# The tail of a fused attention and SwiGLU backward pass: row sums on ScalarE, another order for the last weight gradient, loads cut in quarters

## The chip, the cores and the metric

The kernel runs on one core of a Trainium2 chip. The metric is the device time of one execution in microseconds (us). Three executions of the kernel before took 1677.09, 1677.39 and 1687.07 us; their median is 1677.39. A fourth execution was taken by the hardware profiler.

## The reference

The forward pass is `x + A(xn) + B(xn)`, with `xn = layernorm(x)` over rows of D = 448, S = 2048 rows. A is attention with 16 heads of 28; B is a SwiGLU block with F = 1792. The kernel computes the output and, from `grad_out`, the gradients of x and of the five weight matrices:

```python
xn = _layernorm(x, axis=-1)
return x + _A_ref(xn, A_wqkv, A_wo) + _B_ref(xn, B_w_gate, B_w_up, B_w_down)
...
_out, _vjp = jax.vjp(_f, A_x, A_wqkv, A_wo, B_w_gate, B_w_up, B_w_down)
_grads = _vjp(grad_out)
```

Two of these results are finished in the tail that the change touches:

- the gradient of `wqkv`, which is `xn^T` times the gradient of queries, keys and values;
- the gradient of x. With g the gradient that reaches xn, one row of it is `rstd * (g - mean(g) - xn * mean(g * xn)) + dy`, so each row needs the sum of g and the sum of g * xn.

## The kernel before, in words

The work is cut into 16 row tiles of 128 rows (t) and 4 groups of four heads (g). A forward part (lines 497 to 548) computes attention, with the SwiGLU block's matmuls filled in between. A backward part (lines 764 to 859) runs over pairs of heads, blocks of keys and queries; into it go jobs such as the output rows, the two SwiGLU parts of the input gradient (stored in DRAM as pA_d and pB_d, rows of 448 in bf16) and the wqkv gradient of groups 0, 1 and 2. Every engine executes its instructions in the order in which the program issues them; nothing reorders them. SP issues most DMAs, POOL many stores, ScalarE one large load. Waits are semaphores that the framework derives from tiles: a buffer of a pool (`bufs=3` means three) is reused only when its readers are done. DMAs take eight semaphores in turn, so a DMA also waits for the one that had its semaphore eight DMAs earlier.

The tail is lines 865 to 921:

- **Loads.** `dy_t` (all 16 tiles of grad_out, 1792 KB) is loaded in one DMA from ScalarE's queue (L870). `pab` holds pA and pB for all tiles, each loaded in two halves of 896 KB by SP (L874). `dq_c`, three buffers, holds the gradient of queries, keys and values of two row tiles (768 KB); chunk ck is loaded at L880, chunks 0 and 1 ahead of everything, chunk t/2 + 2 at each even t.
- **The last wqkv gradient (group 3).** For each of four row blocks c of the weight (128 rows of D), `dwq_mms` (L615) issues 32 matmuls for keys and values (kvm, L622) and then 32 for queries (qm, L627) into one PSUM tile; they read `dkv_sp` and `dq_sp`, transposed by DMA at L707 and L765. `dwq_out` (L634) copies the result on ScalarE (L637), sorts it on POOL (L644) and stores it from POOL (L645). So block 0's queries stand ahead of block 1's keys and values.
- **The tile loop, t = 0 to 15.** TensorE adds pA and pB by two matmuls with an identity (L896) and 12 matmuls of dq_c with the transposed wqkv (L898) in a PSUM tile (pool ps_sd, three buffers of two banks). VectorE copies it to `g_sb` and sums it (s1, L902), multiplies it with xn and sums that (junk, s2, L906), makes the two columns bb and cc (L910, L912); ScalarE computes `t1 = g_sb * rstd + bb` (L915); VectorE adds `xn * cc` (t2, L917); POOL adds dy (dx, L920); SP stores dx (L921).

Nothing overlaps two tiles on VectorE except by order: the next tile's L902 is issued after this tile's L917, which waits for ScalarE.

Of the kernel before, what the change touches and what calls it, by code (L numbers as in the profile page):

```python
# [9 lines left out]
ACT = mybir.ActivationFunctionType  # L10
ALU = mybir.AluOpType
AX = mybir.AxisListType
FP32 = mybir.dt.float32
BF16 = mybir.dt.bfloat16
# [4 lines left out]
D = 448  # L19
# [3 lines left out]
G = 4  # L23
HP = 32
P = 128
NT = S // P
# [11 lines left out]
def kernel(  # L38
# [19 lines left out]
    pe, act, dve, pool, sp = nc.tensor, nc.scalar, nc.vector, nc.gpsimd, nc.sync  # L58
    ctx.enter_context(tc.manual_schedule())
    x_d = A_x.rearrange("b (t p) d -> p (b t) d", p=P)  # L60
    dy_d = grad_out.rearrange("b (t p) d -> p (b t) d", p=P)
# [14 lines left out]
    pA_d = dram.tile([P, NT, D], BF16, name="pA_d")  # L76
    pB_d = dram.tile([P, NT, D], BF16, name="pB_d")
    dqkv_d = dram.tile([NT // 2, P, 3 * G, 2 * P], BF16, name="dqkv_d")
# [7 lines left out]
    rstd = const.tile([P, NT], FP32, name="rstd")  # L86
    rl_all = const.tile([P, NT, H], FP32, name="rl_all")
    xn_sp = const.tile([P, NT, DP], BF16, name="xn_sp")
# [40 lines left out]
    for c, (d0, dn) in enumerate(DCH):  # L129
        pool.tensor_copy(  # L130
            out=wq_sb[:dn, c].rearrange("p t g (hh r) -> p t (g hh) r", r=HP)[:, :, :, :DH],
            in_=wst[:dn, c, :].rearrange("p (t h d) -> p t h d", t=3, h=H))
# [4 lines left out]
    for hh in range(4):  # L137
        pool.dma_start(out=wo_pad[HP * hh:HP * hh + DH, :, :D], in_=wo_v[hh])
    dve.tensor_reduce(
        out=r_ones[:], in_=ident_f[:].rearrange("p (a b) -> p a b", b=HP)[:, :, 28:30],  # L140
# [49 lines left out]
    for b in range(5):  # L190
        if b < 4:
            bs = slice(4 * b, 4 * b + 4)
            for i in range(4):
                t = 4 * b + i
# [4 lines left out]
            for i in range(4):  # L199
                t = 4 * b + i  # L200
                dve.tensor_scalar(out=xn_sp[:, t, :D], in0=x_b[b][:, i, :],
                                  scalar1=mv[:, t, 0:1], scalar2=rstd[:, t:t + 1],
                                  op0=ALU.subtract, op1=ALU.mult)
# [4 lines left out]
        if b > 0:  # L208
            for tq in range(3):
                m = proj_unit(0, tq, b - 1, "act" if tq == 0 else "dve")  # L210
# [32 lines left out]
    for b in range(4):  # L243
        sp.dma_start_transpose(
            out=dyT[:, 4 * b:4 * b + 4].rearrange("p t c s -> p (t c) s"),
            in_=dy_sp[:, 4 * b:4 * b + 4, :].rearrange("p t d -> p (t d)"))
# [309 lines left out]
    ps_sd = cst.enter_context(tc.tile_pool(name="ps_sd", bufs=3, space=PSUM))  # L556
# [58 lines left out]
    def dwq_mms(g, c, ps):  # L615

        out = []
        lhs = lambda t: xn_sp[:, t, c * P:(c + 1) * P]

        def kvm(t):  # L620
            for hp in range(2):
                pe.matmul(ps[:, hp * P:(hp + 1) * P], lhsT=lhs(t), rhs=dsp[2 * g + hp][0][:, t, :],  # L622
                          start=(t == 0 and hp == 0), stop=(t == NT - 1), skip_group_check=True)

        def qm(t):
            for hp in range(2):
                pe.matmul(ps[:, 256 + hp * 64:256 + hp * 64 + 64], lhsT=lhs(t),  # L627
                          rhs=dsp[2 * g + hp][1][:, t // 8, t % 4, t % 8 // 4, :],
                          start=False, stop=(t == NT - 1), skip_group_check=True)
        for f in (kvm, qm):  # L630
            out += [lambda t=t, f=f: f(t) for t in range(NT)]
        return out

    def dwq_out(g, c, ps):  # L634
        d0, dn = DCH[c]
        o = outp.tile([P, 384], BF16, name="dwq_raw")
        act.copy(out=o[:], in_=ps[:, :384])  # L637
        z = outp.tile([P, 3, 4, DH], BF16, name="dwq_z")
        kv = o[:, :256].rearrange("p (h v j r) -> p h v j r", h=2, v=2, r=HP)
        for tq in range(3):  # L640
            for hp in range(2):
                src = (o[:, 256 + 64 * hp:320 + 64 * hp].rearrange("p (j r) -> p j r", r=HP) if tq == 0
                       else kv[:, hp, 2 - tq])
                pool.tensor_copy(out=z[:, tq, 2 * hp:2 * hp + 2, :], in_=src[:, :, :DH])  # L644
        pool.dma_start(  # L645
            out=out_2[d0:d0 + dn, :].rearrange("p (t c) -> p t c", t=3)[:, :, g * 4 * DH:(g + 1) * 4 * DH],
            in_=z[:dn].rearrange("p t h d -> p t (h d)"))

    def job_mms(i, ps):
        j = jobs[i]  # L650
        if j[0] == "dwq":
            return dwq_mms(j[1], j[2], ps)
        if j[0] == "y":
            t, x = chunk[i]
            out = []
            for n in range(NFC + G):
                rhs = (wo_pad[:, n, :D] if n < G else wtile["wd"][:, n - G, :])
                out.append(lambda n=n, rhs=rhs: pe.matmul(ps[:, :D], lhsT=t[:, n, :], rhs=rhs,
                                                          start=(n == 0), stop=False))
            out.append(lambda: pe.matmul(ps[:, :D], lhsT=ident_bf[:], rhs=x[:], start=False, stop=True))  # L660
            return out
        t = chunk[i]
        w = wtile[("wg", "wu")[j[1]]]
        return [lambda n=n: pe.matmul(ps[:, :D], lhsT=t[:, n, :], rhs=w[:, n, :],  # L664
                                      start=(n == 0), stop=(n == NFC - 1)) for n in range(NFC)]
# [114 lines left out]
    for k in range(N + 2 * UW):  # L780
# [45 lines left out]
        if 1 <= k <= N:  # L826
# [5 lines left out]
            if qi not in TQ:  # L832
                sp.dma_start_transpose(out=dsT[:, :, :, qi * P:(qi + 1) * P].rearrange("p j c q -> p (j c) q"),
                                       in_=DS[k - 1][:].rearrange("p j c -> p (j c)"))
# [30 lines left out]
    with ExitStack() as fin:  # L865
        ckf = fin.enter_context(tc.tile_pool(name="ckf", bufs=3))
        wk = fin.enter_context(tc.tile_pool(name="wk", bufs=3))
        one = fin.enter_context(tc.tile_pool(name="one", bufs=1))
        dy_t = one.tile([P, NT, D], BF16, name="dy_t")
        act.dma_start(out=dy_t[:], in_=dy_d)  # L870
        pab = [one.tile([P, NT, D], BF16, name=f"pab{i}") for i in range(2)]
        for i, src in enumerate((pA_d, pB_d)):
            for hf in range(2):
                sp.dma_start(out=pab[i][:, 8 * hf:8 * hf + 8, :], in_=src[:, 8 * hf:8 * hf + 8, :])  # L874
        dq_c = {}

        def load_c(ck):
            if ck < NT // 2:
                dq_c[ck] = ckf.tile([P, 3 * G, 2 * P], BF16, name="dq_c")
                sp.dma_start(out=dq_c[ck][:], in_=dqkv_d[ck])  # L880
        load_c(0)
        load_c(1)
        for c in range(4):
            ps = ps_sd.tile([P, 2, 512], FP32, name="sd")
            for f in dwq_mms(3, c, ps[:, 0, :]):
                f()
            dwq_out(3, c, ps[:, 0, :])
        wq = wtile["wq"]
        for t in range(NT):
            if t % 2 == 0:  # L890
                load_c(t // 2 + 2)
            cks = dq_c[t // 2]
            g_t = ps_sd.tile([P, 2, 512], FP32, name="sd")
            g_ps = g_t[:, 0, :D]
            for i in range(2):
                pe.matmul(g_ps, lhsT=ident_bf[:], rhs=pab[i][:, t, :], start=(i == 0), stop=False)  # L896
            for n in range(3 * G):
                pe.matmul(g_ps, lhsT=cks[:, n, (t % 2) * P:(t % 2 + 1) * P], rhs=wq[:, n, :],  # L898
                          start=False, stop=(n == 3 * G - 1))
            g_sb = wk.tile([P, D], FP32, name="g_sb")  # L900
            s1 = wk.tile([P, 1], FP32, name="s1")
            dve.tensor_scalar(out=g_sb[:], in0=g_ps, scalar1=1.0, scalar2=None, op0=ALU.mult, op1=ALU.add,  # L902
                              accum_out=s1[:])
            junk = wk.tile([P, D], FP32, name="junk")
            s2 = wk.tile([P, 1], FP32, name="s2")
            dve.scalar_tensor_tensor(out=junk[:], in0=g_sb[:], scalar=1.0, in1=xn_sp[:, t, :D],  # L906
                                     op0=ALU.mult, op1=ALU.mult, accum_out=s2[:])
            bb = wk.tile([P, 1], FP32, name="bb")
            cc = wk.tile([P, 1], FP32, name="cc")
            dve.scalar_tensor_tensor(out=bb[:], in0=s1[:], scalar=-1.0 / D, in1=rstd[:, t:t + 1],  # L910
                                     op0=ALU.mult, op1=ALU.mult)
            dve.scalar_tensor_tensor(out=cc[:], in0=s2[:], scalar=-1.0 / D, in1=rstd[:, t:t + 1],  # L912
                                     op0=ALU.mult, op1=ALU.mult)
            t1 = wk.tile([P, D], FP32, name="t1")
            act.activation(out=t1[:], in_=g_sb[:], func=ACT.Identity, scale=rstd[:, t:t + 1], bias=bb[:, 0:1])  # L915
            t2 = wk.tile([P, D], FP32, name="t2")
            dve.scalar_tensor_tensor(out=t2[:], in0=xn_sp[:, t, :D], scalar=cc[:, 0:1], in1=t1[:],  # L917
                                     op0=ALU.mult, op1=ALU.add)
            dx = wk.tile([P, D], BF16, name="dx")
            pool.tensor_tensor(out=dx[:], in0=t2[:], in1=dy_t[:, t, :], op=ALU.add)  # L920
            sp.dma_start(out=out1_d[:, t, :], in_=dx[:])  # L921
# [31 lines left out]
```

## Time and profile before

| what | before |
|---|---|
| median of three runs | 1677.39 us |
| the profiled execution, its own time | 1683.64 us |
| its span | 1681.9 us |
| TensorE (PE) busy, of the span | 1519.8 us (90%) |
| ScalarE (ACT) busy | 1186.3 us (71%) |
| VectorE (DVE) busy | 1131.8 us (67%) |
| GpSimd (POOL) busy | 400.9 us (24%) |
| mean granted clock of TensorE | 0.952 |
| last wqkv gradient, first matmul | at 1596.86 us |
| first tile of the loop, first matmul | at 1615.53 us |
| last dx on POOL, start | at 1675.38 us |

How to read it. Busy shares are means over stages with different limits; the tail is the last 85 us, and there the timeline is read, line by line: start, duration, engine, line of the kernel, operation, tiles written and read, shape and count, and in brackets the idle time of the engine before it and what ended that. PEld is TensorE's load of weights, which runs beside its matmuls. A queue (SPq, ACTq, POOLq) shows the issue of a DMA, not its transfer. In rows by stretches of time, the granted clock of TensorE stands as a share of full speed, the DMA column is the mean busy share of the 16 DMA engines, and GB/s is what they moved.

### The profile page before, as it was taken

The page shows a single profiled execution, that of the slowest core. Times are in us where ns is not written, and L with a number is a line of the kernel's source. Part 1 is how long each engine was busy: PE and PEld are TensorE (multiplying, and loading weights), DVE is VectorE, ACT ScalarE, POOL GpSimd, SP SyncE. Part 2 cuts the span into 40 slices and gives each one's busy share as a digit, 9 for nine tenths or more (in the row PEclk, how much of TensorE's full clock was granted, in tenths as well). Part 3 has the DMA queues.
Part 4 walks back from the last instruction along what each step waited for, and adds up shares of the span by engine and source line. Part 5 has one row for each costly group of instructions (what it writes and reads, how often), then busy time and mean ns, then how long its engine had stood idle before and what let it go on. Part 6 is the DMA issues. An engine that isn't in the chain of part 4 may idle for free. (4 is left out here: it accounts for less than half of the span.)

```text
span 1681.9 us, 32121 instructions
## 1 busy us (share of the span) xinstructions
PE 1519.8 (90%) x12176; PEld 600.7 (36%) x12176; DVE 1131.8 (67%) x1530; ACT 1186.3 (71%) x1346; POOL 400.9 (24%) x664
## 2 busy tenths in 40 slices
PE   3699999999999999696998999999989999999875
PEld 1132333333233333232443335443335433544352
DVE  6365555555555456345887788888878888888736
ACT  2497888888777678574776777777777777777611
POOL 4133334344234333421001101010102101111132
PEclk9699999999998899797999989999999999999998
DMA  4785658687866577548999999999999999999963
GB/s 126 145 181 115 133 121 169 140 169 118 157 131 130 124 136 148 138 93 231 214 208 212 196 175 196 207 196 208 206 202 194 202 202 179 175 195 195 175 239 100
DMA packets 682155, 285.13 MB, mean 170 GB/s; under 512 B 637792, under 2 KB 651088, under 8 KB 682000
## 3 DMA queue, kind: packets, MB, share of 16 engines
q1 hardware_dynamic: 653616, 215.74, 68.7%
q0 software_dynamic: 25808, 64.30, 15.4%
q10 hardware_dynamic: 2576, 3.04, 0.6%
q8 instruction: 95, 1.56, 0.4%
q14 instruction: 60, 0.49, 0.1%
HBM read 67.34 MB, written 63.44 MB: 78 GB/s over the span
## 5 line engine op out<-in xcount | busy, mean ns | idle before, releaser
L831 DVE TENSOR_TENSOR ds<-sd,E 128x1024 bf16<-128x1024 f32 x512 | 607.6, 1217 | 81.5 <-PE sd L814 34.2
L819 ACT ACTIVATE E<-sd 128x1024 bf16<-128x1024 f32 x512 | 520.1, 1031 | 193.4 <-PE sd L814 99.0
L535 ACT ACTIVATE eT<-s_ps 128x1024 bf16<-128x1024 f32 x512 | 518.2, 1025 | 159.8 <-PE s_ps L531 154.5
L801 PE MATMUL sd<-KV,QD 32*128 32x512 bf16 x1024 | 202.1, 391 | 19.2 <-DVE ds L831 8.1
L814 PE MATMUL sd<-KV,QD 32*128 32x512 bf16 x1024 | 202.9, 388 | 10.9 <-DVE ds L831 6.8
L694 PE MATMUL acc<-ds,Qsp 128*32 128x512 bf16 x1024 | 204.5, 395 | 1.2 <-DVE ds L831 1.2
L531 PE MATMUL s_ps<-qT,kT 32*128 32x512 bf16 x1024 | 204.7, 397 | 0.0
L694 PE MATMUL acc<-E,dOsp 128*32 128x512 bf16 x1024 | 204.3, 395 | 0.0
L339 PE MATMUL f_ps<-xnT,wgu 128*128 128x512 bf16 x448 | 135.9, 400 | 24.7 <-DVE w_sb L365 13.0
L378 POOL DMA_DIRECT2D hd_d<-fT x168 | 126.9, 769 | 40.9 <-DVE fT L363 24.9
L531 PEld LDWEIGHTS <-kT 32*128 32x128 bf16 x1024 | 48.2, 91 | 203.7 <-issue 201.7
L664 PE MATMUL aux<-W,ck 128*128 128x448 bf16 x448 | 106.6, 354 | 6.9 <-DVE dsT L730 6.9
L313 PE MATMUL f_ps<-xn_sp,f_sp 128*128 128x448 bf16 x448 | 110.6, 355 | 0.0
L709 POOL DMA_DIRECT2D dqkv_d<-dkv_o x64 | 39.2, 617 | 284.9 <-ACT dkv_o L700 284.8
L801 PEld LDWEIGHTS <-QD 32*128 32x128 bf16 x1024 | 50.2, 91 | 149.0 <-issue 140.5
L511 PE MATMUL o_ps<-eT,v_sp 128*32 128x512 bf16 x1024 | 101.7, 399 | 0.0
L730 DVE COPY dsT<-aux 128x512 bf16<-128x512 bf16 x128 | 54.3, 424 | 61.7 <-ACT dsT L728 61.7
L694 PEld LDWEIGHTS <-dOsp 128*32 128x32 bf16 x1024 | 50.3, 94 | 120.3 <-issue 117.3
L814 PEld LDWEIGHTS <-QD 32*128 32x128 bf16 x1024 | 69.4, 91 | 53.4 <-issue 34.2
L721 PE MATMUL aux<-ident_bf,ds 128*128 128x128 bf16 x1024 | 78.5, 219 | 11.0 <-DVE dq_acc L758 3.5
L743 PE MATMUL aux<-dsT,Ksp 128*32 128x512 bf16 x1024 | 78.3, 405 | 4.1 <-DMA dsT<-ds 2.5
L351 DVE SCALAR_TENSOR_TENSOR g<-t_sb,f_ps 128x512 f32<-128x512 f32 x56 | 38.4, 686 | 64.6 <-ACT t_sb L349 64.5
(130 smaller groups left out, 1803.1 us busy)
## 6 DMA issues: line engine op xcount, KB each, us to landing
hd_d<-fT POOLq DMA_DIRECT2D x168, 128.0 KB, 4.0
ck<-hd_d SPq DMA_DIRECT2D x32, 448.0 KB, 4.2
ck<-hd_d SPq DMA_DIRECT2D x16, 576.0 KB, 5.0
dsT<-ds SPq DMA_TRANSPOSE x384, 4.1
dq_c<-dqkv_d SPq DMA_DIRECT2D x8, 768.0 KB, 4.7
dqkv_d<-dkv_o POOLq DMA_DIRECT2D x64, 64.0 KB, 3.5
W<-wT_d SPq DMA_DIRECT2D x14, 224.0 KB, 3.9
out_dram<-dw_o POOLq DMA_DIRECT2D x28, 96.0 KB, 4.1
```

The lines of the kernel that those rows point to most:

```text
L313: pe.matmul(acc[:, :D], lhsT=src[:, 12 * (t // 4) + 4 * wi + t % 4, :], rhs=rhs[:, t, :D], start=(t == 0), stop=(t == NT - 1))
L339: pe.matmul(st[name][:], lhsT=w(c), rhs=src[:, tsl, c, :], start=(c == 0), stop=(c == 3))
L378: pool.dma_start(out=hd_d[tsl, :, G + NFC * wi + fc, :].rearrange("k p s -> p k s"), in_=o[:, wi, :].rearrange("p (k s) -> p k s", k=4))
L511: pe.matmul(o_ps[HP * hh:HP * (hh + 1), :], lhsT=v[:, kt, HP * hh:HP * (hh + 1)], rhs=e[hh // 2][:, hh % 2, :], start=(kt == 0), stop=(kt ...
L531: pe.matmul(s_ps[:, j, :], lhsT=kT[r:r + HP, kt * P:(kt + 1) * P], rhs=qT[r:r + HP, qc * 512:(qc + 1) * 512], start=True, stop=True, tile_ ...
L535: act.activation(out=e[:], in_=s_ps[:], func=ACT.Exp, scale=SCALE)
L664: return [lambda n=n: pe.matmul(ps[:, :D], lhsT=t[:, n, :], rhs=w[:, n, :], start=(n == 0), stop=(n == NFC - 1)) for n in range(NFC)]
L694: pe.matmul(acc[r:r + HP, :], lhsT=src[:, qt, 64 * hp + HP * j:64 * hp + HP * j + HP], rhs=m[:, j, :], start=(qt == 0), stop=(qt == NT - 1 ...
L801: pe.matmul(s_ps[:, j, :], lhsT=q[HP * j:HP * j + HP, qt * P:(qt + 1) * P], rhs=kv[HP * j:HP * j + HP, kc * 512:(kc + 1) * 512], start=Tru ...
L814: pe.matmul(d_ps[:, j, :], lhsT=q[r:r + HP, qt * P:(qt + 1) * P], rhs=kv[r:r + HP, kc * 512:(kc + 1) * 512], start=True, stop=True, tile_p ...
L819: act.activation(out=E[k][:], in_=s_ps[:], func=ACT.Exp, scale=SCALE)
L831: dve.tensor_tensor(out=DS[k - 1][:], in0=d_ps[:], in1=E[k - 1][:], op=ALU.mult)
```

## The change

- `dwq_mms` returns its two parts apart. In the tail, the keys' and values' part of all four blocks is issued first, then the queries' part of each block followed by its `dwq_out`. The four blocks take two PSUM tiles instead of four, two blocks in the two banks of one. The jobs of groups 0, 1 and 2 join the two parts and keep their order.
- dy_t, pA and pB are loaded in quarters of four tiles (448 KB each), inside `load_c` ahead of the even chunks of dq_c: quarter 0 with chunk 0, quarter 1 with chunk 2 (issued at t = 0), quarter 2 with chunk 4 (at t = 4), quarter 3 with chunk 6 (at t = 8). dy's quarters are issued from ScalarE's queue, so at t = 0, 4 and 8 in front of ScalarE's work on that tile.
- s1 is summed by ScalarE, in an Identity activation from PSUM that writes a bf16 `g_sb` that nothing reads. VectorE's junk and ScalarE's t1 read PSUM instead of g_sb. The PSUM tile is therefore held until t1 is done.

Lines of the changed kernel: loads L880, L881, L883; matmuls L905, L907; g_sb L911; junk L914; bb L918; cc L920; t1 L923; t2 L925; dx L928; store L929.

```diff
         for f in (kvm, qm):
-            out += [lambda t=t, f=f: f(t) for t in range(NT)]
+            out.append([lambda t=t, f=f: f(t) for t in range(NT)])
         return out
...
         if j[0] == "dwq":
-            return dwq_mms(j[1], j[2], ps)
+            return sum(dwq_mms(j[1], j[2], ps), [])
...
-        act.dma_start(out=dy_t[:], in_=dy_d)
         pab = [one.tile([P, NT, D], BF16, name=f"pab{i}") for i in range(2)]
-        for i, src in enumerate((pA_d, pB_d)):
-            for hf in range(2):
-                sp.dma_start(out=pab[i][:, 8 * hf:8 * hf + 8, :], in_=src[:, 8 * hf:8 * hf + 8, :])
...
         def load_c(ck):
-            if ck < NT // 2:
-                dq_c[ck] = ckf.tile([P, 3 * G, 2 * P], BF16, name="dq_c")
-                sp.dma_start(out=dq_c[ck][:], in_=dqkv_d[ck])
+
+            if ck >= NT // 2:
+                return
+            if ck % 2 == 0:
+                ts = slice(2 * ck, 2 * ck + 4)
+                for i, src in enumerate((pA_d, pB_d)):
+                    sp.dma_start(out=pab[i][:, ts, :], in_=src[:, ts, :])
+                act.dma_start(out=dy_t[:, ts, :], in_=dy_d[:, ts, :])
+            dq_c[ck] = ckf.tile([P, 3 * G, 2 * P], BF16, name="dq_c")
+            sp.dma_start(out=dq_c[ck][:], in_=dqkv_d[ck])
         load_c(0)
         load_c(1)
+        mms = []
         for c in range(4):
-            ps = ps_sd.tile([P, 2, 512], FP32, name="sd")
-            for f in dwq_mms(3, c, ps[:, 0, :]):
-                f()
-            dwq_out(3, c, ps[:, 0, :])
+            if c % 2 == 0:
+                g_t = ps_sd.tile([P, 2, 512], FP32, name="sd")
+            mms.append((g_t[:, c % 2, :], dwq_mms(3, c, g_t[:, c % 2, :])))
+        for part in range(2):
+            for c, (ps, m) in enumerate(mms):
+                for f in m[part]:
+                    f()
+                if part == 1:
+                    dwq_out(3, c, ps)
...
-            g_sb = wk.tile([P, D], FP32, name="g_sb")
+            g_sb = wk.tile([P, D], BF16, name="g_sb")
             s1 = wk.tile([P, 1], FP32, name="s1")
-            dve.tensor_scalar(out=g_sb[:], in0=g_ps, scalar1=1.0, scalar2=None, op0=ALU.mult, op1=ALU.add,
-                              accum_out=s1[:])
+            act.activation(out=g_sb[:], in_=g_ps, func=ACT.Identity, accum_out=s1[:])
...
-            dve.scalar_tensor_tensor(out=junk[:], in0=g_sb[:], scalar=1.0, in1=xn_sp[:, t, :D],
+            dve.scalar_tensor_tensor(out=junk[:], in0=g_ps, scalar=1.0, in1=xn_sp[:, t, :D],
...
-            act.activation(out=t1[:], in_=g_sb[:], func=ACT.Identity, scale=rstd[:, t:t + 1], bias=bb[:, 0:1])
+            act.activation(out=t1[:], in_=g_ps, func=ACT.Identity, scale=rstd[:, t:t + 1], bias=bb[:, 0:1])
```

## The prediction

> **What bounds the kernel now.** I read the share of busy time first, then the chain that ended last, then the timeline of the last 90 us, where every changed line lies. TensorE is busy 90% over the whole span, but the last three of the page's 40 slices read 8, 7, 5 for it, so the tail has limits of its own. The profiled execution took 1683.64 us with a span of 1681.9; the median of the three runs is 1677.39 (1677.09 to 1687.07). I work the saving out in the times of the profiled execution and take it off the median unchanged, because the tail is only 5% of the time.
>
> The tail has two parts. Ahead of the tile loop (timeline; start, duration, engine, in brackets the idle time before and its releaser):
>
> ```profile
> 1599.58 0.84 SPq L874 DMA_DIRECT2D pab<-pA_d  x2
> ...
> 1601.93 10.62 SPq L880 DMA_DIRECT2D dq_c<-dqkv_d  x3
> 1605.67 0.96 PE L627 MATMUL sd<-dq_sp,xn_sp 128*128 128x64 bf16 x15 [5.75 <-DMA dq_sp<-dq_o]
> ...
> 1615.53 0.54 PE L896 MATMUL sd<-pab,ident_bf 128*128 128x448 bf16 x2
> ...
> 1618.90 3.99 PE L898 MATMUL sd<-W,dq_c 128*128 128x448 bf16 x12 [2.82 <-DMA dq_c<-dqkv_d]
> ...
> 1622.92 0.62 DVE L902 TENSOR_SCALAR_CACHE_REDUCE g_sb<-sd 128x448 f32<-128x448 f32 x1 [25.27 <-PE sd L898]
> ```
>
> TensorE starts the last wqkv gradient at 1596.86, stops 5.75 us for the transposed queries' part (dq_sp), restarts, reaches the first input-gradient tile at 1615.53, and there waits 2.82 us for dq_c. The first tile's product is complete at 1622.92, when VectorE starts. The stretches of 2 us say why dq_c is late (columns: length, busy time of PE, PEld, DVE, ACT, POOL, granted clock, DMA share, GB/s):
>
> ```profile
> 1602.00:1604.00 2.00, 0.00 (x0) 0.00 (x0) 0.00 (x0) 0.00 (x0) 0.00 (x0) 1.00 1.11 276
> ...
> 1606.00:1608.00 2.00, 2.00 (x27) 2.00 (x25) 0.00 (x0) 0.48 (x1) 0.74 (x5) 0.50 1.01 400
> ...
> 1610.00:1612.00 2.00, 2.00 (x46) 2.00 (x43) 0.00 (x0) 0.48 (x1) 1.08 (x6) 1.00 1.02 409
> ...
> 1618.00:1620.00 2.00, 1.10 (x4) 0.44 (x5) 0.00 (x0) 0.00 (x0) 1.61 (x7) 0.66 1.01 408
> ```
>
> The DMA engines are full from 1600 to 1620: 1792 KB of dy_t, four halves of pab at 896 KB and then dq_c. The clock falls to 0.50 after the 5.75 us pause, and the first tile, after the second pause, takes 3.99 us for its 12 matmuls where later ones take 2.43.
>
> In the loop, a tile in its steady state:
>
> ```profile
> 1633.31 0.54 PE L896 MATMUL sd<-pab,ident_bf 128*128 128x448 bf16 x2
> ...
> 1635.96 0.54 PE L896 MATMUL sd<-pab,ident_bf 128*128 128x448 bf16 x2
> ...
> 1642.10 0.62 DVE L902 TENSOR_SCALAR_CACHE_REDUCE g_sb<-sd 128x448 f32<-128x448 f32 x1
> 1642.26 1.03 POOL L920 TENSOR_TENSOR dx<-t,dy_t 128x448 bf16<-128x448 f32 x1 [2.28 <-DVE t L917]
> ...
> 1642.75 1.02 DVE L906 SCALAR_TENSOR_TENSOR junk<-g_sb,xn_sp 128x448 f32<-128x448 f32 x1
> ...
> 1643.70 0.15 DVE L910 SCALAR_TENSOR_TENSOR bb<-s,rstd 128x1 f32<-128x1 f32 x1
> ...
> 1643.95 0.76 ACT L915 ACTIVATE t<-g_sb,bb,rstd 128x448 f32<-128x448 f32 x1 [2.55 <-DVE bb L910]
> ...
> 1644.81 0.68 DVE L917 SCALAR_TENSOR_TENSOR t<-xn_sp,cc,t 128x448 f32<-128x448 bf16 x1 [0.83 <-ACT t L915]
> 1645.41 0.62 DVE L902 TENSOR_SCALAR_CACHE_REDUCE g_sb<-sd 128x448 f32<-128x448 f32 x1
> ```
>
> The two TensorE lines are 2.65 us apart: that is its price per tile when nothing holds it. The lines from L902 to the next L902 make a ring of 3.31 us: g_sb to junk 0.65, junk to bb 0.95, bb to ScalarE's t1 0.25, t1 to t2 0.86, t2 to the next g_sb 0.60. The ring on VectorE and ScalarE sets the loop, not TensorE. junk takes 1.02 us while POOL adds dx beside it; the first junk, at 1623.59 with POOL idle, took 0.62.
>
> **The change, part by part.** F is the time at which TensorE ends a tile.
>
> Order of the last wqkv gradient. The same 256 matmuls run, keys and values of all four row blocks first. Block 0 keeps its 2.40 us (1596.86 to 1599.26); a block at full clock takes 1.80 (1612.81 to 1614.60). 1596.86 + 2.40 + 3 x 1.80 = 1604.66. The queries' part of a block is 0.93 (1611.88 to 1612.81). Two blocks now share one PSUM tile, and the built instruction list shows a new wait for ScalarE ahead of the second of each pair: queued behind it is all of TensorE. Its price: from the start of such a part (1609.16) to the end of ScalarE's copy (1610.35 + 0.48) is 1.67, plus 0.06 back to TensorE, so 1.73 instead of 0.93. Queries: 2 x 1.73 + 2 x 0.93 = 5.32, to 1609.98. That dq_sp has landed by its need, 1605.1, is likely, as it queued against 1792 KB of dy_t and now against 448; at its old landing it would cost 0.55. I take 0. POOL is paced by the landing of dwq_z (up to 6.4 us) and may reach the first dx 2 us late; three buffers cover that.
>
> Loads by quarters. Ahead of dq_c now lie one quarter each of pA, pB (0.46 MB) on SP and dy on ScalarE's queue: with dq_c 2.16 MB. At 364, 276 and 350 GB/s (1600 to 1606) 1.98 MB pass by 1606, so dq_c lands by 1606.5 to 1609, before its need at 1610.36. The first tile then runs without the pause and warm: 0.38 + 2.43 = 2.81, F of tile 0 = 1612.79 instead of 1622.92. Saved: 10.1 us.
>
> ScalarE's sum. Removed per tile: VectorE's 0.62 g_sb. Added: ScalarE's Identity with a sum. The nearest row for the copy is this one:
>
> ```profile
> L673 ACT CAST row_o<-aux 128x448 bf16<-128x448 f32 x48 | 25.4, 528 | 0.7
> ```
>
> 0.53 us. No row shows ScalarE's read of its sum: at least VectorE's 0.08, at most a whole 4-element ACTIVATE, 0.30 (L197); I take 0.20, between. t1 now reads PSUM: 0.53 to 0.76; I keep 0.76, the same instruction's row. In the instruction list junk waits for ScalarE, not for TensorE: the two readers of one PSUM tile take turns, as here (ScalarE's copy, then VectorE's):
>
> ```profile
> 1587.86 0.59 ACT L728 COPY dsT<-aux 128x512 bf16<-128x512 bf16 x1 [0.22 <-PE aux L721]
> ...
> 1588.47 0.42 DVE L730 COPY dsT<-aux 128x512 bf16<-128x512 bf16 x1 [0.18 <-ACT dsT L728]
> ```
>
> So the chain from F: g_sb 0.03 to 0.76, junk at 0.85, bb at 1.40, t1 at 1.65, t2 at 2.51, dx at 3.27. The ring: t1 0.76, g_sb of the next tile 0.76, hand-over 0.09, junk to bb 0.55, bb to t1 0.25 = 2.41. That is below TensorE's 2.65. It assumes junk at 0.62. The bounds are 0.62 and 1.02; I take 0.62, because junk now reads one operand from PSUM like L902, which overlapped dx from 1642.26 on and still took 0.62. The upper end makes the ring 2.81.
>
> The Trainium skill (SBUF — State Buffer, "Who interferes with whom") says that a VectorE instruction competes with GpSimd's reads only if two of its inputs are in SBUF. Old junk had two, new junk has one; by the page the ring is 2.41, by the plain reading of junk's own row 2.81. No run here shows the mixed case yet.
>
> Supply in the loop. SP's order is dx(t-1), then at even t the next dq_c, at t = 4 and 8 behind a pA and a pB quarter. L880 is issued 1.48 after dx starts (1655.51 to 1656.99), so at F + 4.75; alone dq_c lands 4.5 later, of which 2.0 are 0.79 MB at 390 GB/s. Odd chunks: F + 9.25 against a need four tiles on, 4 x 2.65 + 0.38 = 10.98: hidden. Even ones: 1.70 MB take 4.36, so 4.75 + 2.5 + 4.36 = 11.61: late by 0.63, twice, 1.3 us. At 276 GB/s each would be 2.4 late; at 418, 0.3. The four extra SP issues (0.5 us apart) are in that; ScalarE's three extra issues (0.39, L870) fall once each into a ring with 0.24 to spare and three PSUM buffers ahead: 0, at most 1.2.
>
> The Trainium skill (DMA: Bandwidth & Descriptors, "Anatomy of one DMA" and "Bandwidth") speaks against quarters: about 2.0 us fixed per transfer, and batches of 1 MiB or more. Estimated from it, three pieces one after the other take 9.9 us and the two chunks come 3.7 late each: 1665.2 in all. The rows differ: the last loads of the front landed 2.0 to 2.2 us apart at 768 to 896 KB, with no fixed part between them, so I keep 11.61.
>
> Sum: F of tile 15 = 1612.79 + 15 x 2.65 + 1.3 = 1653.8; last dx at 1657.1 instead of 1675.38. Saved 18.3 us (10.1 ahead of the loop, 8.2 in it); what follows the last dx stays. The profiled execution would be 1665.3, the median 1677.39 - 18.3 = 1659.1.
>
> **Rivals.**
> 1. The ring stays the bound because junk keeps 1.02: 1612.79 + 15 x 2.81 + 3.67, and 0.8 for the even chunks, gives the last dx at 1659.4: 1661.4. For it: junk's row beside dx. Against: L902's.
> 2. The loads set the loop: even chunks 2.4 late each (276 GB/s) add 3.5: 1662.6. For it: TensorE already waited up to 1.26 us for dq_c in this loop, and the slack worked out above is negative. Against: 400 GB/s and more in most stretches.
> 3. The front does not start earlier, because dq_c still lands last there: only the loop's 8.2 remain, 1669.2. Against: only 2.16 MB instead of 6.3 are due ahead of it.
> 4. Slower: ScalarE's queue, now on the ring, stalls at the dy loads ahead of tiles 0, 4 and 8, each waiting for an older transfer on its semaphore. This happened to SP:
>
> ```profile
> SPq L880 <- DMA dy_t<-in_grad_out_dram: 9.2, 1, 9.2
> ```
>
> Three such waits are 27.6 us: 1677.39 - 18.3 + 27.6 = 1686.7. It decides from 6.1 us each. Against: what these three loads wait for in the instruction list (dq_sp, the second pA quarter, the fourth dx) is issued many tiles or microseconds earlier.
>
> **How the numbers follow.** Forecast 0.47; rivals 0.18, 0.22, 0.09, 0.04. With 1% (16.8 us, about what a measurement of this kernel can tell from no change) the border is 1660.6, close to the forecast. Faster: 0.42 of the forecast's 0.47, 0.07 of the first rival, 0.06 of the second: 0.55. Slower by over 1% would need 11.7 us in each of rival 4's waits: 0.02. The rest, 0.43, within 1%. Range: with no late chunk and the cheap ends of g_sb and t1 it is 1657.3, and without TensorE's two new waits (1.6) 1655.7; upwards it takes in rivals 1 and 2 and the runs' own spread of some microseconds: 1655 to 1667, leaving out most of rivals 3 and 4.
>
> **What would show it.** Order: no pause over 1 us on TensorE between 1597 and the first tile, two gaps near 0.8 at the second and fourth queries' part. Loads: first L907 within 1 us of L905, F of tile 0 ten microseconds earlier, 12 matmuls in 2.4 to 2.5. Sum: L905 lines 2.65 apart, junk 0.62 beside dx, idle VectorE. Supply: waits for dq_c only ahead of tiles 8 and 12, about 0.6 each. Wrong if junk stays at 1.02, if tiles are 2.8 apart, if the waits for dq_c exceed 2 us, or if ScalarE is seen waiting for a DMA.

## The result, and the profile after

The changed kernel takes 1664.99 us, the median of 6 runs (1662.26 to 1671.58), against 1679.83 for six runs of the kernel before beside it: ratio 0.9902, 95% interval 0.9878 to 0.9927. The forecast was 1659.1 (1655 to 1667); of the 5.9 between, 2.4 are the kernel before itself, 1679.83 here and 1677.39 there. The profiled execution took 1664.19 us (span 1662.4), where 1665.3 was forecast, but 3.24 us of its gain lie ahead of every changed line: its last wqkv gradient starts at 1593.62 instead of 1596.86. So I measure from that first matmul on. "Front" is the time to the end of the first tile's product (read as the start of its first reader), "loop" the time from there to the start of the last dx. Before: 26.06 + 52.46 = 78.52. After: 16.93 + 45.39 = 62.32, so 16.2 us are saved, 9.1 in the front and 7.1 in the loop, where 18.3 = 10.1 + 8.2 were forecast. What follows the last dx is about 6.5 us in both.

The front, in the timeline of the changed kernel (start, duration, engine, line, tiles; idle time before and its releaser):

```profile
1593.62 8.92 PE L622 MATMUL sd<-dkv_sp,xn_sp 128*128 128x128 bf16 x128
...
1602.38 1.10 PE L627 MATMUL sd<-dq_sp,xn_sp 128*128 128x64 bf16 x32
...
1604.10 2.03 PE L627 MATMUL sd<-dq_sp,xn_sp 128*128 128x64 bf16 x64 [0.62 <-ACT dwq_raw L637]
...
1606.77 1.09 PE L627 MATMUL sd<-dq_sp,xn_sp 128*128 128x64 bf16 x32 [0.64 <-ACT dwq_raw L637]
...
1607.70 0.54 PE L905 MATMUL sd<-pab,ident_bf 128*128 128x448 bf16 x2
...
1608.08 2.43 PE L907 MATMUL sd<-W,dq_c 128*128 128x448 bf16 x12
```

The keys' and values' part of all four blocks now runs in one piece, 8.76 us (1593.62 to 1602.38). The queries' parts take 5.32 to 1607.70, with two waits of 0.62 and 0.64 for ScalarE's copy. There is no pause for dq_sp or dq_c, and the first tile's 12 matmuls take 2.43, where they took 3.99 behind a pause of 2.82.

The stretches of 2 us (length; busy PE, PEld, DVE, ACT, POOL; granted clock; DMA share; GB/s) show two things, the clock at the start and the DMA engines in the loop:

```profile
1594.00:1596.00 2.00, 2.00 (x22) 2.00 (x20) 0.42 (x1) 0.00 (x0) 1.20 (x2) 0.50 0.47 88
1596.00:1598.00 2.00, 2.00 (x30) 2.00 (x28) 0.00 (x0) 0.00 (x0) 0.00 (x0) 0.75 1.21 312
...
1612.00:1614.00 2.00, 2.00 (x13) 1.03 (x11) 0.89 (x3) 1.31 (x3) 1.70 (x9) 1.00 0.02 8
1614.00:1616.00 2.00, 2.00 (x12) 1.02 (x11) 1.33 (x5) 0.88 (x2) 1.70 (x5) 1.00 0.21 53
```

The clock is a mean over the stretch: in stretches of half a microsecond it is 0.50 until 1597.0 and 0.98 to 1.00 from there, in the middle of the keys' and values' part. From 1612 on the DMA engines have little to do for over 6 us (shares 0.02, 0.21 and 0.20 until 1618): the next loads, chunk 3 and then a quarter of pA and pB with chunk 4, lie on SP behind stores of dx. Chunk 3 is issued at 1618.46, the quarter at 1623.75.

One tile of the loop, in the timeline of the changed kernel:

```profile
1622.14 0.62 DVE L914 SCALAR_TENSOR_TENSOR junk<-sd,xn_sp 128x448 f32<-128x448 f32 x1
1622.31 1.03 POOL L928 TENSOR_TENSOR dx<-t,dy_t 128x448 bf16<-128x448 f32 x1 [1.70 <-DVE t L925]
...
1622.69 0.67 DVE L918 SCALAR_TENSOR_TENSOR bb<-s,rstd 128x1 f32<-128x1 f32 x1
...
1623.45 0.72 ACT L923 ACTIVATE t<-sd,bb,rstd 128x448 f32<-128x448 f32 x1 [1.48 <-DVE cc L920]
...
1624.27 0.69 DVE L925 SCALAR_TENSOR_TENSOR t<-xn_sp,cc,t 128x448 f32<-128x448 bf16 x1 [0.85 <-ACT t L923]
...
1625.04 1.04 POOL L928 TENSOR_TENSOR dx<-t,dy_t 128x448 bf16<-128x448 f32 x1 [1.70 <-DVE t L925]
```

From dx to dx 2.73 us, where it was 3.31. junk takes 0.62 beside dx, as hoped, but now bb (128x1) takes 0.67 instead of 0.15 and ends at 1623.36, just after dx (1622.31 + 1.03 = 1623.34). ScalarE's t1 waits for it. So the ring runs through POOL: dx 1.03, hand-over 0.11, t1 0.72 and 0.10, t2 and the way to the next dx 0.77 = 2.73. ScalarE's read of its sum takes 0.20.

The one wait for a load in the loop, at tile 8, with the issue of its chunk, and the start of tile 12, in the same timeline:

```profile
1624.83 0.32 SPq L883 DMA_DIRECT2D dq_c<-dqkv_d  x1
...
1631.21 2.44 PE L907 MATMUL sd<-W,dq_c 128*128 128x448 bf16 x12 [1.53 <-DMA dq_c<-dqkv_d]
...
1641.82 2.43 PE L907 MATMUL sd<-W,dq_c 128*128 128x448 bf16 x12
```

Chunk 4 lands 6.3 us after its issue; TensorE stood for 1.53. No other tile waits for a load: chunk 6, of tile 12, is issued at 1636.06 and lands 5.5 later, at about 1641.6, just ahead of its first matmul. And POOL's way into the loop, the third block's sorted copy and the first dx:

```profile
1611.31 1.08 POOL L644 COPY dwq_z<-dwq_raw 128x56 bf16<-128x56 bf16 x6 [3.06 <-ACT g_sb L911]
...
1615.32 1.07 POOL L928 TENSOR_TENSOR dx<-t,dy_t 128x448 bf16<-128x448 f32 x1
1615.36 1.53 DVE L925 SCALAR_TENSOR_TENSOR t<-xn_sp,cc,t 128x448 f32<-128x448 bf16 x1 [0.67 <-ACT t L923]
```

The third block's sorted copy starts 4.1 us after the second's is done (1606.12 + 1.12), 3.06 of it idle. The two buffers of dwq_z are the reason (the twelfth run shows it); the profile names another releaser. So the first dx starts 4.8 after the first tile's end (1610.51; its first reader starts at 1610.55), not 3.27, and the second tile's t2 takes 1.53 beside it instead of 0.69.

### The profile page after: what moved, and what is told of

Its sections match the earlier page's. It is cut to its first block, busy times and chain, and to the rows that moved or that the text cites. A ratio compares the mean times of both kernels' runs of the same rounds, so it can differ in the third digit from the quotient of the medians.

```text
span 1662.4 us, 32143 instructions
## 1 busy us (share of the span) xinstructions
PE 1513.0 (91%) x12176; PEld 597.6 (36%) x12176; DVE 1123.0 (68%) x1498; ACT 1195.1 (72%) x1378; POOL 400.9 (24%) x664
## 3 DMA queue, kind: packets, MB, share of 16 engines
q0 software_dynamic: 25808, 64.30, 15.3%
## 5 line engine op out<-in xcount | busy, mean ns | idle before, releaser
L728 ACT COPY dsT<-aux 128x512 bf16<-128x512 bf16 x128 | 76.2, 595 | 10.0 <-PE aux L721 7.6
```

The lines of the kernel that those rows point to most:

```text
L728: act.copy(out=dst[:, 0], in_=ps[:, 0:4, :])
```

## The experiments

My theory after the result: each part does what was forecast, loads and sum carry the gain, the loop's step of 2.73 is bb held by POOL's dx, and the loads are a second bound close behind. Rivals: that the order carries the front; that the step is the serial reading of PSUM (e5 leaves that as it is); that the wait at tile 8 is the loss (e9 and e10).

| run | median us (runs) | ratio to before [95%] | front | loop | sum |
|---|---|---|---|---|---|
| before, profiled | | | 26.06 | 52.46 | 78.52 |
| changed | 1664.99 (6) | 0.9902 [0.9878, 0.9927] | 16.93 | 45.39 | 62.32 |
| e1 loads alone | 1672.09 (10) | 0.9954 [0.9926, 0.9982] | 18.15 | 53.12 | 71.27 |
| e2 order alone | 1684.43 (10) | 1.0015 [0.9996, 1.0035] | 27.20 | 52.48 | 79.68 |
| e3 sum alone | 1671.20 (10) | 0.9962 [0.9937, 0.9987] | 24.66 | 43.88 | 68.54 |
| e4 loads and sum | 1667.58 (9) | 0.9911 [0.9886, 0.9937] | 16.83 | 47.85 | 64.68 |
| e5 columns by a row scalar | 1663.61 (4) | 0.9891 [0.9863, 0.9919] | 15.38 | 48.61 | 63.99 |
| e6 junk from SBUF | 1670.52 (1) | | 15.32 | 49.92 | 65.24 |
| e7 earlier loads | 1662.40 (4) | 0.9894 [0.9856, 0.9933] | 15.32 | 45.95 | 61.27 |
| e8 dx twice | 1671.59 (1) | | 15.90 | 50.27 | 66.17 |
| e9 four chunks | 1663.91 (4) | 0.9907 [0.9872, 0.9942] | 15.32 | 45.96 | 61.28 |
| e10 three edits together | 1657.86 (6) | 0.9867 [0.9843, 0.9891] | 16.16 | 42.89 | 59.05 |
| e11 e10's loop, old order | 1663.46 (6) | 0.9903 [0.9878, 0.9928] | 20.30 | 42.90 | 63.20 |
| e12 four dwq_z | 1668.74 (1) | | 16.32 | 45.58 | 61.90 |

Front and loop are each from one profiled execution; in e8 the loop goes to the first of the last tile's two dx. The intervals of the changed kernel, e4, e5, e7, e9, e10 and e11 overlap, so what sets these apart is read from traces. The front needs care there. In the changed kernel, e5, e6, e7, e8, e9 and e12, which share its order, it is the keys' and values' part plus 8.16 to 8.17, and only that part moves: 7.15 to 7.21 where the clock is 1.00 throughout (e5, e6, e7, e9), 7.73 in e8, 8.16 in e12 and 8.76 in the changed kernel. In the last three the granted clock is 0.50 at first (for about 1.2, 2.1 and 3.4 us). So up to 1.6 us of front between two of these runs is clock, not the edit.

**e1, e2, e3: one part each, put into the kernel before.** The diffs are the three parts of the change.

> The kernel before with the loads by quarters alone. Two stretches are measured: the front, from the first matmul of the last wqkv gradient to the end of the first input-gradient tile (26.06 us before, 16.93 after the whole change), and the loop, from there to the start of the last dx (52.46 before, 45.35 after). Theory A, the loads make the front: the transposed queries' part lands about 5 us after the first matmul (as in the changed kernel) instead of 8.8, dq_c is there in time, the pauses go: front 16.5 to 17.5, loop 52.5 with its ring of 3.31 us, total about 9 us faster than before. Theory B, the order makes the front: the 5.75 us pause stays, only the wait for dq_c and the slow first tile go, front about 22, total about 4 us faster.

> The kernel before with the new order of the last wqkv gradient alone. Theory A: dq_c still lands behind 6.3 MB, 22 us after the first matmul, so the wait only moves: front 25.5 to 27 us, loop 52.5, total within 1 us of before. Theory B: the pause of 5.75 us is won: front about 20 us, total 5 to 6 us faster.

> The kernel before with ScalarE's sum alone (junk and t1 read PSUM). Theory A: front 26 us as before; the ring on VectorE and ScalarE goes from 3.31 to about 2.73 us, loop 44 to 46 us, 7 to 8 us faster. Rival, the supply of dq_c sets the loop as soon as the ring is shorter: waits for dq_c at every second tile, loop 48 us or more, at most 4 us faster.

In the traces, loads alone save 7.25 us (7.9 in the front, -0.7 in the loop), the sum alone 10.0 (1.4 and 8.6), the order alone loses 1.2. The three add up to 16.1, close to the 16.2 of the whole, though not place by place: the sum changes nothing in the front, so its 1.4 there is what single executions differ by, and e3's loop is 1.5 shorter than the changed kernel's. The medians say less: the loads' and the sum's intervals lie below 1, the order's takes in 1.

For the front theory A of e1 and e2 came true a little beyond its figures (18.15 and 27.20), and so did that of e3 for the loop (43.88). e3, with all of pA, pB and dy loaded ahead, never waits for a load behind the first tile: its chunk 4 is issued 12.63 after the first tile's end, in the changed kernel 14.28, and lands 5.2 later instead of 6.3. bb is held in both (steps of 2.73), so the 1.5 are about the wait of 1.53 at tile 8.

In e1, in the old order, TensorE's wait for dq_sp shrinks from 5.75 to two short ones of 1.14 and 1.50. In e2 it goes away, and what was hidden behind it shows instead: 3.79 us of waiting for pab at 1614.69 and then, in the timeline of e2,

```profile
1618.97 4.66 PE L904 MATMUL sd<-W,dq_c 128*128 128x448 bf16 x12 [3.75 <-DMA dq_c<-dqkv_d]
```

3.75 for dq_c, with the first tile's 12 matmuls at 4.66 behind it, nearly twice their 2.43. A wait taken away in one place came back in another. In e1 the wait comes back at tile 8, as 0.71 for pab and 1.93 for dq_c.

**e4: loads and sum, without the order.**

> The changed kernel with the old order of the last wqkv gradient: loads by quarters and ScalarE's sum stay. Theory A: the order costs two waits for ScalarE of 0.63 us and saves one pause of about 2.2 us, so front 16.5 to 17.5, loop 45 to 45.5: within 1 us of the changed kernel, about 16 us faster than before. Theory B: front about 22, some 5 us slower than the changed kernel, about 11 us faster than before.

Tile 8 in the timeline of e4:

```profile
1633.07 4.05 PE L900 MATMUL sd<-W,dq_c 128*128 128x448 bf16 x12 [1.80 <-DMA dq_c<-dqkv_d]
```

The front is 16.83, no longer than with the new order (16.93): dq_sp came 2.92 late and nothing else was lost. But e4's granted clock was 1.00 from its first matmul on, and the changed kernel's was not. Beside the new order at full clock (15.32 to 15.38 in e5, e6, e7 and e9) the old one is 1.5 longer. The loop is longer by 2.5, and tile 8 explains it: a wait of 0.70 for pab, one of 1.80 for dq_c, and then 12 matmuls in 4.05; one step from dx to dx is 6.47. So theory A has the front but not the loop (45 to 45.5). That loss is the loads': the issue of pA took 2.11 instead of 0.42, and why the profile doesn't show.

**e5: bb and cc without a second tensor operand.**

```diff
-dve.scalar_tensor_tensor(out=bb[:], in0=s1[:], scalar=-1.0 / D, in1=rstd[:, t:t + 1],
-                         op0=ALU.mult, op1=ALU.mult)
+dve.tensor_scalar(out=bb[:], in0=s1[:], scalar1=rstd[:, t:t + 1], scalar2=-1.0 / D,
+                  op0=ALU.mult, op1=ALU.mult)
```

(cc likewise.)

> The changed kernel, with bb and cc computed by tensor_scalar, which takes rstd as a per-row scalar instead of as a second tensor. In the changed kernel bb (128x1) takes 0.67 us instead of 0.15 whenever POOL's dx runs beside it, and ends when dx ends, so that the ring goes dx, bb, t1, t2, dx: 2.73 us per tile. Theory, bb is held because its two tensor inputs are in SBUF while POOL reads SBUF: bb falls to 0.15 beside dx, the ring to about 2.4, tiles follow TensorE at 2.65, the loop is 1 to 1.5 us shorter than the changed kernel's apart from its wait for dq_c. Rival, bb waits for something else that ends then (the read of the sum, any VectorE access beside POOL): bb stays at 0.6 to 0.67 and tiles at 2.73.

dx, bb and the longest wait, in the timeline of e5:

```profile
1620.88 1.03 POOL L928 TENSOR_TENSOR dx<-t,dy_t 128x448 bf16<-128x448 f32 x1 [1.24 <-DVE t L925]
...
1621.27 0.21 DVE L918 TENSOR_SCALAR bb<-s,rstd 128x1 f32<-128x1 f32 x1
...
1631.88 4.07 PE L907 MATMUL sd<-W,dq_c 128*128 128x448 bf16 x12 [2.73 <-DMA dq_c<-dqkv_d]
```

bb takes 0.21 in the middle of dx, and dx follows dx in 2.28 where the loop catches up; that is the ring without the hold. On TensorE's pace the steps are 2.65. The loop is longer all the same: waits of 1.01 (at 1623.68, chunk 3) and 2.73 for dq_c, the second with 12 matmuls in 4.07 behind it. Chunk 3 was late because POOL was: the first dx starts 6.9 after the first tile's end (4.8 in the changed kernel), SP issues the chunk behind the second dx, 9.4 after that end instead of 7.9, and it lands 5.1 later. Chunk 4 was issued as in the changed kernel (14.4 and 14.3) but took 8.4 to land instead of 6.3; why is not shown.

**e6: junk reads the bf16 copy in SBUF** (its sum is then of rounded values).

```diff
-dve.scalar_tensor_tensor(out=junk[:], in0=g_ps, scalar=1.0, in1=xn_sp[:, t, :D],
+dve.scalar_tensor_tensor(out=junk[:], in0=g_sb[:], scalar=1.0, in1=xn_sp[:, t, :D],
```

> The changed kernel, with junk reading ScalarE's bf16 copy g_sb in SBUF instead of PSUM (s2 is then summed from rounded values). Theory, the hold by dx is passed on: junk is slowed to 1.0 us and ends about with dx, and bb behind it then takes 0.15, so that tiles stay at 2.6 to 2.8 us and the loop within 1 us of the changed kernel's. Rival, the 0.4 us that junk saved by reading PSUM went into the ring in full: tiles at 3.1, loop 5 to 6 us longer.

Tile by tile the timeline of e6 shows this:

```profile
1625.18 0.62 DVE L914 SCALAR_TENSOR_TENSOR junk<-g_sb,xn_sp 128x448 f32<-128x448 bf16 x1
...
1625.34 1.35 POOL L928 TENSOR_TENSOR dx<-t,dy_t 128x448 bf16<-128x448 f32 x1 [1.70 <-DVE t L925]
...
1625.72 0.98 DVE L918 SCALAR_TENSOR_TENSOR bb<-s,rstd 128x1 f32<-128x1 f32 x1
```

junk, which starts first, keeps 0.62; dx, which starts 0.16 later, is stretched from 1.03 to 1.35, and bb is held to its end. The step is 3.05 instead of 2.73. The theory is out; the rival has the step (3.1), but by another way, since junk lost nothing itself. So that junk reads PSUM is worth 0.32 per tile, and in this pair whoever starts first of VectorE and POOL keeps its time.

**e7: tiles 8 to 15 of pA, pB and dy right behind chunk 2**, as one half each instead of two quarters.

```diff
-if ck % 2 == 0:
+if ck in (0, 2):
...
+if ck == 2:
+    ts = slice(8, 16)
+    for i, src in enumerate((pA_d, pB_d)):
+        sp.dma_start(out=pab[i][:, ts, :], in_=src[:, ts, :])
+    act.dma_start(out=dy_t[:, ts, :], in_=dy_d[:, ts, :])
```

> The changed kernel, with pA, pB and dy of tiles 8 to 15 loaded in one half each right behind chunk 2 of dq_c instead of as quarters at tiles 4 and 8. Theory, the quarters ahead of chunk 4 cause the wait of TensorE at tile 8 (1.53 us in the changed kernel, 1.80 plus a cooled clock without the new order): no wait for dq_c or pab in the loop, loop 43.5 to 44.5 us against 45.4, front within 0.5 of 16.9. Rival, chunk 4 is late whatever lies ahead of it, since its issue waits for dx of tile 3: a wait of 1 us or more at tile 8 remains, and the loop stays above 45.

A wait of 1.25 for dq_c at tile 8 is still there, as the rival had it. But the run does not clear the quarters. POOL reached the first dx 6.5 after the first tile's end instead of 4.8, so the fourth dx, behind which SP issues chunk 4, came 1.1 later, and the chunk was issued at 14.5 after that end against 14.3 with the quarters ahead of it. It landed 5.6 later instead of 6.3. Three runs together tell the two apart: e12 has the quarters and an early POOL (first dx at 2.9) and waits, e7 has no quarters there and a late POOL and waits, e3 has an early POOL (3.0) and no quarters and does not wait. So in these single executions either is enough. The loop of e7 is 45.95.

**e8: dx issued twice on POOL.**

```diff
 pool.tensor_tensor(out=dx[:], in0=t2[:], in1=dy_t[:, t, :], op=ALU.add)
+pool.tensor_tensor(out=dx[:], in0=t2[:], in1=dy_t[:, t, :], op=ALU.add)
```

> The changed kernel, with POOL's addition dx issued twice (the second writes the same values). POOL is idle 1.7 us per tile, so by its own time this costs nothing but 1.03 us once at the end. Theory, bb is held until POOL's last dx ends: tiles at 2.73 + 1.03 = about 3.75 us, loop about 15 us longer. Rival, POOL's dx does not set the ring: tiles stay at 2.7, loop 1 us longer.

In the timeline of e8 the second dx of one tile, the next tile's bb, and a later wait:

```profile
1622.85 1.45 POOL L929 TENSOR_TENSOR dx<-t,dy_t 128x448 bf16<-128x448 f32 x1
...
1623.87 0.45 DVE L918 SCALAR_TENSOR_TENSOR bb<-s,rstd 128x1 f32<-128x1 f32 x1
...
1628.28 0.93 PE L907 MATMUL sd<-W,dq_c 128*128 128x448 bf16 x2 [2.75 <-DMA dq_c<-dqkv_d]
```

This fell out against the expectation. bb does not wait for both: it ends as the dx in flight ends (1622.85 + 1.45 = 1624.30; 1623.87 + 0.45 = 1624.32), and the other dx runs afterwards. The steps are 2.4 to 2.7, apart from three longer ones around TensorE's waits for loads (5.9, 3.8 and 3.9). Here bb is held for the instruction in flight, not for POOL's whole work; e9 shows another case. The loop lost 4.9 elsewhere: with two dx per tile, the stores and so the issues of the chunks came later, and TensorE waited 2.75 with 12 matmuls in 3.98 behind it.

**e9: a fourth buffer for dq_c, chunks and quarters issued two tiles earlier.**

```diff
-        ckf = fin.enter_context(tc.tile_pool(name="ckf", bufs=3))
+        ckf = fin.enter_context(tc.tile_pool(name="ckf", bufs=4))
...
+        load_c(2)
...
-                load_c(t // 2 + 2)
+                load_c(t // 2 + 3)
```

> The changed kernel, with four buffers for dq_c and every chunk (with its quarters) loaded two tiles earlier. Theory, TensorE's wait at tile 8 goes, but bb behind dx still sets the ring at 2.73 us and POOL still comes late to the first dx, so the loop stays between 44.5 and 45.5 us (45.39 in the changed kernel), and the front at 15.3 to 17. Rival, the loads set the loop: without the wait tiles follow TensorE at 2.65 and the loop falls below 44.

No wait for dq_c is left in the loop, and yet it takes 45.96, a little over the theory's range; the rival is out. POOL's way into it, and the bb beside it, in the timeline of e9:

```profile
1611.50 2.06 POOL L929 TENSOR_TENSOR dx<-t,dy_t 128x448 bf16<-128x448 f32 x2
...
1611.51 2.08 DVE L919 SCALAR_TENSOR_TENSOR bb<-s,rstd 128x1 f32<-128x1 f32 x1
```

POOL reaches the first dx 6.5 after the first tile's end (1604.99). The second dx follows at once, and bb, which started with the first, ends with the second (1613.59 and 1613.56). From there the step of 2.73 cannot make up for the delay. I take this for the loss, not the loads; e10, which takes the hold away, bears it out.

**e10: e5's columns, e9's chunks, and blocks 0 and 2, 1 and 3 paired in a PSUM tile instead of 0 and 1, 2 and 3.**

> The changed kernel with three additions: bb and cc by tensor_scalar, four buffers for dq_c, and the blocks of the last wqkv gradient paired so that the second queries' part does not wait for ScalarE's copy of the first (blocks 0 and 2 share a PSUM tile, and 1 and 3). Theory: no wait for ScalarE in the front (15.5 to 16 us at the clock of the changed kernel's trace, 14 to 15 at that of the later ones), tiles at 2.65 on TensorE's pace, no wait for dq_c, loop 43 to 43.8; tail from the first matmul to the last dx 57.5 to 59.8 us against 62.3 in the changed kernel and 78.5 before; about 19 to 21 us faster than before, ratio 0.988. Rival, one of the three brings another wait (dq_c beside the stores, ScalarE's copies in front of its sums): tail above 61.

The loop is 42.89: dx 2.65 apart, bb 0.21 beside it, one wait for a load, 0.77 for dq_c ahead of tile 0 (in the front). In all 1657.86 us, 0.9867 [0.9843, 0.9891] of the kernel before. The changed kernel's interval overlaps it by a little; in the trace e10's two stretches are 3.3 us shorter. The tail, 59.05, is in the theory's range. POOL was late here too, the first dx 4.9 after the first tile's end, and without the hold of bb the loop made up for it. The pairing itself brought nothing: the waits for ScalarE are gone, but there is a pause of 1.24 behind the first five of the fourth block's 32 matmuls, whose cause the profile doesn't show.

**e11: e10's loop with the old order of the last wqkv gradient.**

> The kernel before with loads by quarters and ScalarE's sum, bb and cc by tensor_scalar and four buffers for dq_c, in the old order of the last wqkv gradient. Theory: the order is worth one pause of 2 to 3 us against the two waits that pairing removes: front 16.5 to 17.5 us, loop 43 to 43.8, tail 59.5 to 61.3, so 1 to 2 us behind the run with all. Rival, the order is worth nothing: tail within 0.5 of it.

The loop is the same, the front 20.30: waits of 1.08 and 3.58 us for dq_sp, and behind them a block of 32 matmuls in 3.19 instead of 1.95. So the order is worth 4.1 here, more than theory and rival had. Beside the new order at full clock it was worth 1.5 in e4 and 2.8 in e1 (18.15 against 15.3). It depends on when dq_sp lands: the waits for it that the old order shows are 2.92 in e4, 2.64 in e1 and 4.66 here, and the new order shows none.

**e12: four buffers for dwq_z**, so that POOL need not wait for a store.

```diff
-        z = outp.tile([P, 3, 4, DH], BF16, name="dwq_z")
+        z = zp.tile([P, 3, 4, DH], BF16, name="dwq_z")
...
+        zp4 = fin.enter_context(tc.tile_pool(name="zp4", bufs=4))
...
-                    dwq_out(3, c, ps)
+                    dwq_out(3, c, ps, zp4)
```

> The changed kernel, but the sorted copy of the last wqkv gradient (dwq_z) has four buffers of its own instead of two, so that POOL need not wait for a store to land before the third block. Theory A (POOL's late start costs time, because a ring of 2.73 us on a TensorE pace of 2.65 never makes up a delay): no idle time of 3 us on POOL ahead of the third block's copies; the first dx starts 3.3 us after the end of the first tile instead of 4.77; the second tile's t2 takes 0.69 instead of 1.53; the second dx starts at 5.6 instead of 6.42, and the loop, measured from the first tile's end to the last dx, is 0.8 us shorter: 44.6 instead of 45.39. Theory B (three buffers cover a late POOL, as I forecast): the first dx may come earlier, but the last does not, and the loop stays at 45.4.

The first dx and the next tile's bb in the timeline of e12:

```profile
1617.85 1.03 POOL L929 TENSOR_TENSOR dx<-t,dy_t 128x448 bf16<-128x448 f32 x1 [1.24 <-DVE t L926]
...
1618.78 0.15 DVE L919 SCALAR_TENSOR_TENSOR bb<-s,rstd 128x1 f32<-128x1 f32 x1
```

The first dx starts 2.94 after the first tile's end (1614.91), and the next two follow 2.65 apart: an early dx is nearly over when bb starts, so bb keeps 0.15 (it starts at 1618.78, dx ends at 1618.88). A longer step (2.83) then brings dx later, and bb is held again, 0.24, 0.32 and then 0.67 up to the wait at tile 8. That POOL's delay goes with four buffers, as theory A had it, held, and at tile 7 the run is 0.7 ahead of the changed kernel. Then chunk 4 is waited for: it lands 20.9 after the first tile's end, in the changed kernel 20.7, and from tile 8 on both are level within 0.2. The loop is 45.58, theory B's number, though not for its reason: the chunk's landing takes the gain back, not three buffers.

## Why the prediction came out as it did

**Order: right but for the clock.** The queries' part took 5.32, the very figure, with 0.62 and 0.64 for the two waits for ScalarE, and dq_sp was in time. "Block 0 keeps its 2.40 us" and 1.80 for each other block gave 7.80; it took 8.76, because the granted clock stayed at 0.50 until 1597. That is all of the front's missing microsecond. The same instructions took 8.16 in e12 and 7.16 in e9, where the clock was 1.00. I credited the order with the 10.1 of the front together with the loads; e1 and e2 give it to the loads (7.9 of it alone), and the order only helps once they are in place.

**Loads ahead of the loop: right.** dq_c was no longer waited for, and the first tile took 2.81.

**ScalarE's sum: the step that failed is the ring of 2.41.** Its parts held: g_sb 0.53 + 0.20, junk 0.62, "junk to bb 0.55", t1 0.72 (forecast 0.76). "bb to t1 0.25" did not; it took 0.76 (1622.69 to 1623.45). I costed bb by its row of 0.15, taken where POOL was just done, and did not ask what was in flight when a shorter junk lets bb start in the middle of dx. The hold that I took off junk fell on bb, and the ring became 2.73, just above TensorE's 2.65. e5 takes it away and gets 2.28. The Trainium skill (SBUF — State Buffer, "Who interferes with whom") had it: an instruction of VectorE with two inputs in SBUF competes with a GpSimd instruction that reads SBUF, while one with at most one such input does not, outside the modes that use both ports. I applied that to junk, where this trace agrees (0.62 with one, and 3.05 per step in e6 with two), and not to bb, which has two of one element per partition.

The cost in this run was small. From tile 8 on there are seven steps of 2.73 instead of 2.65, 0.56 us in all; what the ring cost ahead of tile 8 lies under the wait for chunk 4.

**Supply: the right mechanism, mis-sized for tile 8 and counted once too often.** The forecast had tile 8's chunk land 11.61 after the end of tile 3 by TensorE's pace, 0.63 late; it landed 12.75 after it (1631.21 - 1610.51 - 7.95), so 1.77 late. Of the difference 0.54 stands at pA's issue, at 5.29 instead of 4.75, and the rest behind it. An earlier issue of pA would not have been enough by itself: in e12 it came 0.7 earlier, but pB's issue took 0.80 instead of 0.37, and the chunk landed 0.2 later. That puts tile 8's dx at 26.3 instead of 25.1, which is the whole of the loop's missing 1.1. Tile 12's chunk was not waited for, and the "twice" in the sum was wrong by its own terms. Chunk 6 is issued behind the dx of tile 7, whose product is complete before TensorE waits at tile 8. So that wait puts off the need for chunk 6 and not its issue: it landed about 0.3 before tile 12's first matmul (1641.82) and would have been 1.3 late without the 1.53. The loop's end came out near all the same by luck: the 0.63 forecast for tile 12 and the 0.56 lost to the ring cancel. The skill's figures gave 3.7 late for each (DMA: Bandwidth & Descriptors, "Anatomy of one DMA", which gives them for DMAs issued from GpSimd; these loads are issued from SP and ScalarE); the trace has half of that, once.

**POOL "may reach the first dx 2 us late; three buffers cover that".** It was 1.5 late by my chain of 3.27, and 1.8 by the 2.94 of e12, and the cover was not the buffers. With the ring above TensorE's pace a lateness is not made up for (e9: 6.5 after the first tile, and the loop no shorter without any wait for a load), and a late dx makes SP issue the chunks later (e5). In the changed kernel the late chunk at tile 8 hides it, as e12 shows. Costed at 0, it did cost about 0, for a wrong reason.

**The rivals.** Rival 1 named the right engine and the wrong instruction: junk kept 0.62, but the ring bound the loop at 2.73, near its 2.81. Rival 2 holds for one chunk. Rivals 3 and 4 fell: the front is 9.1 shorter, and ScalarE issues each quarter of dy in 0.38 us with no wait. Between the trace's 16.2 and the forecast's 18.3 lie two terms: 1.0 of clock and 1.1 of chunk 4. Of the 5.9 us between the two times that leaves 1.4, less than the runs of either kernel differ by.

**Open.** Why dq_sp lands so differently from run to run, why the clock is low at the start of the front in some executions, why the issue or landing of chunk 4 is slow in e4, e5 and e12, why a step of 3.0 instead of 2.73 appears at the same place in several runs, and the pause of 1.24 in e10 were not tried. e10 with four buffers for dwq_z was not tried either.

## What to carry to other kernels

When an instruction is made shorter because it no longer competes with another engine, ask what then starts while that other engine is still busy: here the hold moved from a 128x448 product to a 128x1 column that cost 0.15 in the old trace. A ring a few hundredths above the pace of the bounding engine does not recover what it lost at its start; look for such rings even when they cost little per step. And when an engine is made faster, count how much earlier its loads must be issued, not only how long they take: here the DMA engines had little to do while the next loads lay behind stores in one queue, and in several runs an engine off the critical path (POOL) set when they were issued. And before two fronts are compared, compare the clock that they were granted: here it hid what the order was worth.

## What the runs showed of the hardware

- A 128x1 product of two tensors in SBUF on VectorE, 0.15 us alone, is held beside POOL's tensor_tensor: in the changed kernel it took 0.67 and ended with dx. In e8 it ended with the dx in flight (0.45); in e9 it started with the first of two dx in a row and ended with the second (2.08). What decides between the two is not shown. With rstd as a per-row scalar it takes 0.21 beside dx (e5).
- Whoever started first kept its time: junk with two inputs in SBUF took 0.62 when it started 0.16 ahead of dx, and dx took 1.35 instead of 1.03 (e6). In the kernel before, junk started after dx and took 1.02.
- After waits of TensorE of 2.5 us and more in the loop (0.70 + 1.80 in e4, 2.73 in e5, 2.75 in e8) 12 matmuls took 3.98 to 4.07 us, and 4.66 after 0.71 + 1.93 in e1; the granted clock fell to 0.50 in each. After 1.53 (the changed kernel), 1.98 and 0.83 + 1.54 (both e6) they took 2.44.
